# A three-way gate on ScalarE and VectorE: three activations per tile become two, and the maximum becomes a minimum and a maximum

## The chip, the core and the metric

One core of a Trainium2 chip runs the whole program. The metric is the device time of one execution in microseconds. TensorE (PE) multiplies matrices into PSUM, and its weight loads (PEld) are listed apart; ScalarE (ACT) and VectorE (DVE) work elementwise from PSUM or SBUF to SBUF; GpSimd (POOL) fills constants and issues some DMAs; SyncE (SP) issues most of them.

## What is computed

A linear attention with a delta rule over 768 steps gives `x`, 3072 tokens of 384 numbers. A feed-forward layer follows, whose activation has three pieces with `beta = 1`:

```python
h = x @ w_in                      # 3072 x 384 times 384 x 2048
neg = h <= -beta
pos = h >= beta
g = np.where(pos, h, np.where(neg, 0.0, (h + beta) ** 2 / (4.0 * beta)))
return (g @ w_out)                # 3072 x 2048 times 2048 x 384
```

With u = (h + 1) / 2 the middle piece is u squared. u squared is never below h, and it meets h at h = 1 and 0 at h = -1.

## The kernel before

The tokens come in six groups of 512. The attention of a group is made in chunks of 64 steps, by many small products (Gram matrices, a triangular solve on VectorE, a chain of state updates), and each result lands in a tile `xb` as a high and a low part. The feed-forward layer works on the group before: its 2048 hidden units are 16 tiles of 128. One *item* is one such tile for one group, 128x512 numbers; in the first group, 12 items are halves of 128x256. There are 102 items, 90 whole and 12 half.

For each item `up` makes `h` in PSUM (tile `h`, two buffers) with nine products (high and low parts of both factors, three passes over three tiles). The activation makes `s` in SBUF from `h`. `rest` splits `s` into a high part `ghi` (a cast on ScalarE, L807) and a low part `glo` (a subtraction on VectorE, L808), and `down`, two items later (`LAG = 2`), multiplies these with the second weight into the accumulators `o0` to `o3`.

The activation of an item before the change:

```python
relu(s[:, c], h[:, c], mid, -0.5)          # ScalarE, L812 called from L831
...
relu(s[:, c], s[:, c], one, -1.0)          # ScalarE, L812 called from L843
nc.scalar.activation(out=s[:, c], in_=s[:, c], func=AF.Square)                      # L844
...
nc.vector.tensor_tensor(out=s[:, c], in0=h[:, c], in1=s[:, c], op=ALU.max)          # L846
```

That is r = relu(0.5 - 0.5h), then relu(1 - r), which is u cut off below 0 and above 1, then its square, then the maximum with h.

The order of work on each engine is the order in which the code is written: the pools are under a manual schedule, each engine runs its instructions in that order, and semaphores make it wait. Pieces of the attention stand between the items: `pe` holds products for an item's two halves, whose evictions run on ScalarE and VectorE (`finish(evicts)` between the first relu and the second, `finish(late)` ahead of the next item), `fill` holds steps of the solve on VectorE and loads, and in the first group the letters of `FRONT` and `FILL` place the unpacking of the weights (a `grow` and a `cast` on ScalarE, `shift`, `join` and `low` on VectorE). Lines that come up below: L165 products on a zero tile that keep TensorE at work in the opening, L239 a Gram product of K, L370 a transpose of the solve's result into `XT`, L414 the write of the first merge into `XT`, L426 and L441 a product of the second merge and its eviction to `GG`, L476 the eviction to `SU`, L493 the product that reads `SU`, L693 `up`, L708 `down`, L324 and L368 two operations of the solve, L457 and L551 two of the state chain.

Of the kernel before, what the change touches and what calls it, by code (L numbers as in the profile page):

```python
# [7 lines left out]
F32 = mybir.dt.float32  # L8
F32R = mybir.dt.float32r
I32 = mybir.dt.int32  # L10
AF = mybir.ActivationFunctionType
ALU = mybir.AluOpType
# [28 lines left out]
def delta_rule_moe(ctx: ExitStack, tc: tile.TileContext, kqa, kqb, kv, beta, w, out):  # L41
# [14 lines left out]
    nc = tc.nc  # L56
# [5 lines left out]
    P = 128  # L62
# [3 lines left out]
    const = ctx.enter_context(tc.tile_pool(name="const", bufs=1))  # L66
# [104 lines left out]
                                channel_multiplier=-1, compare_op=ALU.is_gt, fill=0.0)  # L171
    mid = const.tile([P, 1], F32, name="half")
    nc.vector.memset(mid, 0.5)
    one = const.tile([P, 1], F32, name="one")
    nc.vector.memset(one, 1.0)
    tiny = const.tile([P, 1], F32, name="tiny")
    nc.vector.memset(tiny, 1e-30)  # L177
    nc.scalar.activation(out=sb.tile([P, 32], F32, name="y0")[:, 0:1], in_=mid, func=AF.Sqrt, bias=tiny)
# [406 lines left out]
    def finish(evicts):  # L585

        for p in [q() for q in evicts]:
            if p:
                p()

    def products(*pieces):
        return [p() for p in pieces]
# [29 lines left out]
    def do(codes):  # L622
        for c in codes:
            if c in "wW":
                weight_loads(tile_[0], tile_[0] + 1, nc.scalar if c == "W" else nc.sync)
                tile_[0] += 1
            elif c == "F":
                dense(1)
            elif c == "l":
                f, g = loads.pop(0)  # L630
                f(g)
            else:
                run(tasks[c], 1)
# [51 lines left out]
    def cols(bs):  # L685
        return slice(bs[0] * NB, bs[-1] * NB + NB)

    def up(G, f, bs):
        h = ps.tile([P, 2 * NB], F32, name="h", bufs=2)
        n = 0  # L690
        for k in range(3):
            for x, y in PASSES:
                nc.tensor.matmul(h[:, cols(bs)], WT[f][:, 0, x, k * P:(k + 1) * P], XB[G][:, y, k, cols(bs)], start=(n == 0), stop=(n == 8))  # L693
                n += 1
        return h

    def down(G, f, bs):
        ghi, glo = gs.pop((G, f, bs))
        for b in bs:
            left[G, b] -= 1  # L700
            for k in (2 * b, 2 * b + 1):
                if (G, k) not in oacc:
                    oacc[G, k] = ps.tile([P, DM], F32, name=f"o{k}")
                    new = True
                else:
                    new = False
                for n, (x, y) in enumerate(PASSES):
                    nc.tensor.matmul(oacc[G, k], (ghi, glo)[x][:, k * P:(k + 1) * P], WT[f][:, 1, y, :],  # L708
                                     start=(new and n == 0), stop=(left[G, b] == 0 and n == 2))

    def store(G, b):
        o = sb.tile([P, 2, DM], F32, name="wx", bufs=2)
        for k in (2 * b, 2 * b + 1):
            nc.scalar.copy(out=o[:, k % 2], in_=oacc[G, k])
            for j in range(CT):
                send(G, k, j, o, nc.sync)
# [79 lines left out]
    def fills(at_):  # L796
        for x, *n in fill.pop(at_, []):
            if x in (load_k, load_q, load_kv, weight_loads):
                x(*n)
            else:  # L800
                run(x, *n)

    def rest(item, s):
        ghi = sb.tile([P, 2 * NB], F32R, name="ghi", bufs=2)
        glo = sb.tile([P, 2 * NB], F32R, name="glo", bufs=2)
        c = cols(item[2])
        nc.scalar.copy(out=ghi[:, c], in_=s[:, c])  # L807
        nc.vector.tensor_tensor(out=glo[:, c], in0=s[:, c], in1=ghi[:, c], op=ALU.subtract)  # L808
        gs[item] = ghi, glo

    def relu(out, in_, bias, scale):
        nc.scalar.activation(out=out, in_=in_, func=AF.Relu, bias=bias, scale=scale)  # L812

    late, last, ready = [], None, []
    for n, item in enumerate(items):
        at_, c = 2 * n, cols(item[2])
        codes = FILL[n].split(",") if n < len(FILL) else [""] * 6
        do(codes[0])
        finish(late)
        do(codes[1])  # L820
        if last:
            rest(*last)
            ready.append(last[0])
        do(codes[2])
        if at_ == 2 * HALF:
            spare.clear()
        assert (item[1], low) in done, item
        h = up(*item)

        s = sb.tile([P, 2 * NB], F32, name="s", bufs=2)  # L830
        relu(s[:, c], h[:, c], mid, -0.5)  # L831
        evicts = products(*pe.pop(at_, []))
        do(codes[3])
        fills(at_)
        finish(evicts)
        do(codes[4])
        if len(ready) == LAG:
            x = ready.pop(0)
            down(*x)
            for b in x[2]:  # L840
                if left[x[0], b] == 0:
                    store(x[0], b)
        relu(s[:, c], s[:, c], one, -1.0)  # L843
        nc.scalar.activation(out=s[:, c], in_=s[:, c], func=AF.Square)  # L844
        late = products(*pe.pop(at_ + 1, []))
        nc.vector.tensor_tensor(out=s[:, c], in0=h[:, c], in1=s[:, c], op=ALU.max)  # L846
        do(codes[5])
        fills(at_ + 1)
        last = item, s
# [53 lines left out]
```

## Time and profile before

| | |
|---|---|
| three runs | 598.97, 602.3, 602.72 us; median 602.3 us |
| profiled execution, from the first to the last instruction | 599.7 us, its own time here |
| mean granted TensorE clock | 0.983 |
| TensorE busy | 581.0 us (97%) |
| its weight loads busy | 502.3 us (84%) |
| ScalarE busy | 396.5 us (66%) |
| VectorE busy | 394.2 us (66%) |

A busy time is the sum over an engine's instructions in that one execution. A wait is an engine's idle time ahead of an instruction, put down to what released it. Times in a listing are microseconds from the start of the span, and a line number is that of the kernel before.

### The profile page before, as it was taken

To read this page: it belongs to the slowest core of one execution; us is meant where nothing else is said; L and a number is where in the kernel's file an instruction comes from. 1 tells how busy PE (TensorE), PEld (TensorE's weight loads), DVE (VectorE), ACT (ScalarE), POOL (GpSimd) and SP (SyncE) were. 2 spreads that over 40 slices of the span, in tenths; PEclk is the share of its full clock that TensorE was granted. 3 is DMA by queue.
4 is the path that set the end of the run, shared out by engine and by line. 5 is a ranking of instruction groups with operands and counts; after the bars stand their busy time and mean duration, and the time that the engine had idled before them with its cause. 6 is when DMAs were issued, how large, how long until landed. Compare 5 with 4: busy or idle time off the path is not lost.

```text
span 599.7 us, 21759 instructions
## 1 busy us (share of the span) xinstructions
PE 581.0 (97%) x9585; PEld 502.3 (84%) x9585; DVE 394.2 (66%) x828; ACT 396.5 (66%) x689; POOL 33.0 (6%) x67
## 2 busy tenths in 40 slices
PE   8898999999999999999999999999999999999996
PEld 7777888788878878888888898888888888898986
DVE  5967899953689943689933689934689925333332
ACT  4538898478756596656586656586656585676663
POOL 6200010000020000020000020000020000000000
PEclk9969799999999999999999999999999999999999
DMA  5682657200333011134011134011143000020001
GB/s 144 207 290 86 205 194 210 66 8 9 93 96 103 8 32 45 31 98 121 13 32 45 33 103 119 8 32 45 34 108 91 1 3 16 15 54 1 0 1 52
DMA packets 32302, 42.77 MB, mean 71 GB/s; under 512 B 7056, under 2 KB 26768, under 8 KB 32208
## 3 DMA queue, kind: packets, MB, share of 16 engines
q1 hardware_dynamic: 31216, 40.41, 23.6%
q8 instruction: 75, 1.23, 0.9%
q0 software_dynamic: 576, 0.57, 0.4%
q10 hardware_dynamic: 416, 0.39, 0.2%
q14 instruction: 19, 0.16, 0.1%
HBM read 34.47 MB, written 4.72 MB: 65 GB/s over the span
## 4 chain that ended last, share of the span: by engine, by line
PE 46%; issue 28%; ACT 13%; DVE 5%; SPq 4%; DMA 3%; POOL 1%; POOLq 0%; ACTq 0%; DVEq 0%
PE o L708 16%; PE h L693 16%; PE ch L493 3%; ACT s L812 2%; ACT GG L441 2%; PE ch L467 2%; ACT XT L443 1%; PE o L165 1%; PE ch L252 1%; PE ch L451 1%; DMA KV<-in_kv_dram 1%; PE ch L566 1%; PE ch L428 1%; ACT s L844 1%; ACT xb L191 1%
## 5 line engine op out<-in xcount | busy, mean ns | idle before, releaser
L693 PE MATMUL h<-xb,wt 128*128 128x512 f32 (+1 forms) x918 | 225.0, 388 | 4.0 <-DVE s L846 2.0
L708 PE MATMUL o<-wt,ghi 128*128 128x384 f32 x768 | 200.7, 343 | 0.0
L693 PEld LDWEIGHTS h<-xb,wt 128*128 128x128 f32 x918 | 162.5, 189 | 38.1 <-DVE s L846 2.8
L708 PEld LDWEIGHTS o<-wt,ghi 128*128 128x128 f32 x768 | 137.8, 189 | 7.0
L846 DVE TENSOR_TENSOR s<-h,s 128x512 f32<-128x512 f32 (+1 forms) x102 | 66.8, 655 | 116.3 <-ACT s L844 115.4
L708 PE MATMUL o<-wt,glo 128*128 128x384 f32 x384 | 130.1, 339 | 0.3 <-DVE glo L808 0.3
L807 ACT CAST ghi<-s 128x512 fp32r<-128x512 f32 (+1 forms) x102 | 60.9, 597 | 102.9 <-DVE s L846 87.7
L808 DVE TENSOR_TENSOR glo<-s,ghi 128x512 fp32r<-128x512 f32 (+1 forms) x102 | 66.6, 653 | 39.2 <-ACT ghi L807 39.2
L812 ACT ACTIVATE s<-h,half 128x512 f32<-128x512 f32 (+1 forms) x102 | 67.4, 661 | 35.9 <-PE h L693 35.4
L708 PEld LDWEIGHTS o<-wt,glo 128*128 128x128 f32 x384 | 72.6, 189 | 1.1 <-DVE glo L808 1.1
L812 ACT ACTIVATE s<-s,one 128x512 f32<-128x512 f32 (+1 forms) x102 | 71.7, 703 | 2.4
L844 ACT ACTIVATE s<-s 128x512 f32<-128x512 f32 (+1 forms) x102 | 61.9, 607 | 3.2
L360 DVE TENSOR_TENSOR pr<-A 128x30 f32<-128x30 f32 (+14 forms) x120 | 39.3, 327 | 7.0 <-POOL A L325 5.1
L362 DVE TENSOR_TENSOR A<-A,pr 128x30 f32<-128x30 f32 (+14 forms) x120 | 39.8, 332 | 4.4
L165 PE MATMUL o<-wx 128*128 128x512 f32 x87 | 28.9, 479 | 1.5 <-DVE tiny L177 1.5
L493 PEld LDWEIGHTS ch<-Q,SU 64*64 64x64 f32 (+3 forms) x1056 | 22.4, 135 | 4.4 <-ACT ghi L807 1.5
L493 PE MATMUL ch<-Q,SU 64*64 64x64 f32 (+3 forms) x1056 | 24.7, 222 | 0.7 <-ACT SU L476 0.7
L165 PEld LDWEIGHTS o<-wx 128*128 128x128 f32 x87 | 18.8, 227 | 5.8 <-DVE tiny L177 1.5
L325 POOL TENSOR_SCALAR_AFFINE_SELECT A<-A 128x1024 f32<-128x1024 f32 x4 | 5.1, 1264 | 300.0 <-DMA xb<-X 256.4
L266 DVE TENSOR_TENSOR Q<-ch,mask 64x512 f32<-64x512 f32 (+1 forms) x30 | 20.6, 687 | 0.4
L426 PEld LDWEIGHTS ch<-XT,GG 32*32 32x32 f32 x704 | 12.4, 106 | 5.3 <-issue 2.8
L441 ACT ACTIVATE GG<-ch 32x512 f32<-32x512 f32 x22 | 12.9, 588 | 5.0 <-PE ch L426 4.7
(159 smaller groups left out, 575.2 us busy)
## 6 DMA issues: line engine op xcount, KB each, us to landing
wt<-in_w_dram SPq DMA_DIRECT2D x16, 768.0 KB, 6.0
out_dram<-wx SPq DMA_DIRECT2D x44, 96.0 KB, 2.2
KV<-in_kv_dram SPq DMA_DIRECT2D x36, 96.0 KB, 2.5
KV<-in_kv_dram SPq DMA_DIRECT2D x72, 48.0 KB, 2.4
KV<-in_kv_dram SPq DMA_DIRECT2D x12, 192.0 KB, 2.9
xb<-X SPq DMA_DIRECT2D x60, 32.0 KB, 2.0
K<-in_kqb_dram SPq DMA_DIRECT2D x12, 128.0 KB, 2.6
Q<-in_kqb_dram SPq DMA_DIRECT2D x12, 128.0 KB, 2.8
```

What stands on the lines that cost most here:

```text
L165: nc.tensor.matmul(warm_ps, warm[:, 0:P], warm, start=True, stop=True)
L360: nc.vector.tensor_tensor(out=pr, in0=A[:, 0:n, j:j + 1].broadcast_to([P, n, m]), in1=A[:, j:j + 1, j + 1:32].broadcast_to([P, n, m]), op= ...
L362: nc.vector.tensor_tensor(out=A[:, 0:n, j + 1:32], in0=A[:, 0:n, j + 1:32], in1=pr, op=ALU.add)
L441: nc.scalar.mul(out=GG[r:r + 32, ga, :, 0:32], in_=y1[r:r + 32], mul=-1.0)
L493: nc.tensor.matmul(yy[i][o * C:o * C + C, e, p], SF[rows, u:u + C], w_[rows, x, k, :], **how)
L693: nc.tensor.matmul(h[:, cols(bs)], WT[f][:, 0, x, k * P:(k + 1) * P], XB[G][:, y, k, cols(bs)], start=(n == 0), stop=(n == 8))
L708: nc.tensor.matmul(oacc[G, k], (ghi, glo)[x][:, k * P:(k + 1) * P], WT[f][:, 1, y, :], start=(new and n == 0), stop=(left[G, b] == 0 and n ...
L807: nc.scalar.copy(out=ghi[:, c], in_=s[:, c])
L808: nc.vector.tensor_tensor(out=glo[:, c], in0=s[:, c], in1=ghi[:, c], op=ALU.subtract)
L812: nc.scalar.activation(out=out, in_=in_, func=AF.Relu, bias=bias, scale=scale)
L844: nc.scalar.activation(out=s[:, c], in_=s[:, c], func=AF.Square)
L846: nc.vector.tensor_tensor(out=s[:, c], in0=h[:, c], in1=s[:, c], op=ALU.max)
```

## The change

The first relu takes the other sign of its scale, so that it gives relu(0.5h + 0.5), which is u cut off below 0 only. The second relu and its constant tile `one` are gone. The square is then taken of a number that may exceed 1, and VectorE takes the minimum of it with 1 ahead of the maximum with h, both in one scalar_tensor_tensor. In the changed kernel that operation stands on L840, the square on L838, the relu on L826.

```diff
-    one = const.tile([P, 1], F32, name="one")
-    nc.vector.memset(one, 1.0)
...
-    def relu(out, in_, bias, scale):
-        nc.scalar.activation(out=out, in_=in_, func=AF.Relu, bias=bias, scale=scale)
-
...
-        relu(s[:, c], h[:, c], mid, -0.5)
+        nc.scalar.activation(out=s[:, c], in_=h[:, c], func=AF.Relu, bias=mid, scale=0.5)
...
-        relu(s[:, c], s[:, c], one, -1.0)
         nc.scalar.activation(out=s[:, c], in_=s[:, c], func=AF.Square)
         late = products(*pe.pop(at_ + 1, []))
-        nc.vector.tensor_tensor(out=s[:, c], in0=h[:, c], in1=s[:, c], op=ALU.max)
+        nc.vector.scalar_tensor_tensor(out=s[:, c], in0=s[:, c], scalar=1.0, in1=h[:, c], op0=ALU.min, op1=ALU.max)
```

Engine by engine the instructions keep their order; 102 of ScalarE's and one memset of VectorE's are left out. One place stands for all: ScalarE's queue in the fifth group, from the eviction of the first merge to the evictions to `SU`. Before:

```order
L807 CAST ghi<-s 128x512
L812 ACTIVATE s<-h,half 128x512
L433 COPY XT<-ch 32x16x32 x2
L441 ACTIVATE GG<-ch 32x16x32 x2
L443 COPY XT<-XT 32x16x32 x2
L812 ACTIVATE s<-s,one 128x512
L844 ACTIVATE s<-s 128x512
L807 CAST ghi<-s 128x512
L812 ACTIVATE s<-h,half 128x512
L476 COPY SU<-ch 64x384 x2
```

And now, the same stretch:

```order
L805 CAST ghi<-s 128x512
L826 ACTIVATE s<-h,half 128x512
L431 COPY XT<-ch 32x16x32 x2
L439 ACTIVATE GG<-ch 32x16x32 x2
L441 COPY XT<-XT 32x16x32 x2
L838 ACTIVATE s<-s 128x512
L805 CAST ghi<-s 128x512
L826 ACTIVATE s<-h,half 128x512
L474 COPY SU<-ch 64x384 x2
```

The second relu between the eviction to `XT` and the square is left out; the rows around it keep their places.

## Rows read from the trace of the kernel before

**Rows 1.** The page, busy time of the engines.
```profile
PE 581.0 (97%) x9585; PEld 502.3 (84%) x9585; DVE 394.2 (66%) x828; ACT 396.5 (66%) x689; POOL 33.0 (6%) x67
```

**Rows 2.** Busy times by stretch: start:end, length, busy us of each engine.
```profile
52.00:594.90 542.90, 534.21 (x8508) 465.65 (x8506) 357.63 (x736) 369.12 (x640) 18.34 (x33) 0.99 0.21 58
...
75.00:120.00 45.00, 42.49 (x821) 35.86 (x817) 43.55 (x86) 32.87 (x55) 3.11 (x6) 1.00 0.50 156
180.00:210.00 30.00, 29.86 (x324) 26.21 (x322) 28.02 (x62) 16.99 (x27) 0.00 (x0) 1.00 0.22 55
```

**Rows 3.** TensorE's waits and their releasers: us in total, times, longest us.
```profile
PE h L693 <- DVE s L846: 2.0, 3, 1.0
...
PE ch L426 <- DVE XT L414: 1.1, 1, 1.1
PE ch L426 <- DVE XT L370: 0.9, 1, 0.9
...
PE ch L239 <- ACT GG L441: 0.8, 4, 0.3
PE ch L493 <- ACT SU L476: 0.7, 1, 0.7
```

**Rows 4.** ScalarE's groups by shape: busy us, mean ns, idle before.
```profile
L812 ACT ACTIVATE s<-s,one 128x512 f32<-128x512 f32 x90 | 65.5, 728 | 2.2
...
L812 ACT ACTIVATE s<-s,one 128x256 f32<-128x256 f32 x12 | 6.2, 513 | 0.2
```

**Rows 5.** VectorE's groups by shape.
```profile
L846 DVE TENSOR_TENSOR s<-h,s 128x512 f32<-128x512 f32 x90 | 61.7, 686 | 112.4 <-ACT s L844 111.7
...
L551 DVE TENSOR_TENSOR xb<-ch,xb 128x384 fp32r<-128x384 f32 x22 | 11.1, 547 | 0.0
L457 DVE TENSOR_TENSOR KV<-KV,ch 128x384 f32<-128x384 f32 x21 | 10.7, 547 | 1.7 <-PE ch L451 1.7
...
L368 DVE TENSOR_TENSOR A<-A,gm 128x1024 f32<-128x1024 f32 x4 | 4.9, 1220 | 0.0
L324 DVE SCALAR_TENSOR_TENSOR A<-A,gm 128x1024 f32<-128x1024 f32 x4 | 4.9, 1214 | 0.0
```

**Rows 6.** ScalarE in order of time at 488 us: start us, us, instruction.
```profile
488.15 0.72 ACT L812 ACTIVATE s<-s,one 128x512 f32<-128x512 f32 x1
...
491.58 1.45 ACT L476 COPY SU<-ch 64x384 f32<-64x384 f32 x3
```

**Rows 7.** ScalarE in order of time at 132 us.
```profile
132.15 0.72 ACT L812 ACTIVATE s<-s,one 128x512 f32<-128x512 f32 x1
...
134.75 1.19 ACT L441 ACTIVATE GG<-ch 32x512 f32<-32x512 f32 x2
```

**Rows 8.** VectorE in order of time at 207 us.
```profile
207.70 0.69 DVE L846 TENSOR_TENSOR s<-h,s 128x512 f32<-128x512 f32 x1 [0.18 <-ACT s L844]
```

**Rows 9.** TensorE's weight loads in order of time, near the end.
```profile
592.86 0.19 PEld L708 LDWEIGHTS o<-wt,glo 128*128 128x128 f32 x1 [0.17 <-DVE glo L808]
```

**Rows 10.** VectorE in order of time at 61 us.
```profile
61.18 0.42 DVE L846 TENSOR_TENSOR s<-h,s 128x256 f32<-128x256 f32 x1
...
62.39 0.41 DVE L414 TENSOR_TENSOR XT<-XT,o 128x256 f32<-128x256 f32 x1
```

**Rows 11.** Two of these stretches, L846 alone: start:end, length, VectorE busy, clock.
```profile
75.00:120.00 45.00, 4.94 (x8) 1.00 0.50 156
180.00:210.00 30.00, 4.79 (x7) 1.00 0.22 55
```

**Rows 12.** Stretches around a low clock; the third last column is the granted clock.
```profile
61.70:62.90 1.20, 0.10 (x3) 0.04 (x4) 1.17 (x3) 1.20 (x4) 0.00 (x0) 1.00 0.09 21
...
64.50:71.30 6.80, 6.75 (x82) 6.11 (x82) 6.68 (x14) 5.79 (x12) 0.00 (x0) 0.50 1.02 355
```

**Rows 13.** Chain that ended last, second relus: start us, us; first and last of 12.
```profile
53.42 0.52 ACT s L812
...
431.26 0.62 ACT s L812
```

## The prediction

> **What bounds the kernel now.** I read the page first: TensorE is busy 581.0 of 599.7 us, VectorE and ScalarE 66% each [rows 1]. The change takes work from ScalarE alone, so the question is where TensorE stands still, and for whom. The busy times by stage come next [rows 2]: from the first expert matmul at 52 us to the last at 594.9 us TensorE is busy 534.2 of 542.9 us. That leaves 8.7 us, and whatever a faster ScalarE gives has to come out of these 8.7 us or out of TensorE's clock. The same rows show who is nearly full: VectorE, with 43.55 of 45 us from 75 us on, 28.0 of 30 us from 180 us on, and three more such stretches in the later blocks. ScalarE has 17 of 30 us there. The list of TensorE's waits [rows 3] then names the releasers. The largest are VectorE's: its maximum `s` (L846) 2.0 us in three waits, its writes of `XT` 1.1 and 0.9 us. ScalarE's are small: the eviction to `GG` (L441) 0.8 us in four waits, the eviction to `SU` (L476) 0.7 us in one. So the removed row's engine is not the bound; I look at each wait and ask whether the removed row stands in the queue ahead of its releaser.
>
> **What is removed.** The second relu, 90 rows of 728 ns and 12 of 513 ns [rows 4], is 65.5 + 6.2 = 71.7 us of ScalarE's 396.5 us. The order of the instructions shows that nothing else moves on any engine, so each of these rows can shorten a wait only where it stands between a releaser and what that releaser waited for. The memset of `one`, one column on VectorE, goes too: TensorE's first products wait for loads that land after it, so I count nothing, and without that cover it would be one column's write. The first relu has another sign of its scale, one instruction with the same operands: no change.
>
> **What VectorE's new operation costs.** The trace has no minimum-and-maximum of one SBUF and one PSUM operand, so I bound it by the nearest rows [rows 5]. Today's maximum takes 686 ns for 128x512. That the PSUM operand becomes the second input and not the first changes nothing in the trace: 547 ns with PSUM second (L457), 547 ns with PSUM first (L551), both 128x384. That two operations with a scalar replace one changes nothing either: a scalar_tensor_tensor on 128x1024 takes 1214 ns (L324), a tensor_tensor on the same shape 1220 ns (L368). The lower end is therefore 6 ns in 1220, or 3 ns per operation and 0.3 us over 102 of them; the upper end is that the operation passes one element where today's passes two, which by L324 is 1214 ns. I take 686 ns, since L324 is the same instruction at the rate of a plain one; both ends come back below.
>
> The Trainium skill speaks against that: "Vector Engine (DVE) Microarchitecture Reference", section "Points that are easy to get wrong", says that a scalar_tensor_tensor with two SBUF sources that aren't bf16 runs at half the throughput. The trace does not agree for L324, which has two f32 sources in SBUF and is no slower than L368; and the new operation has only one source in SBUF. By that rule VectorE would get the load of the first rival below; by the row it gets none.
>
> **What it is worth, wait by wait.**
> - At 492 us TensorE waits 0.7 us for the eviction to `SU` [rows 3]. Back from it on ScalarE stand the first relu, the cast to `ghi` that waited for VectorE's maximum, the square, and the second relu at 488.15 us, with no wait for anything else between [rows 6]. All of them come about 0.75 us earlier, the row's 0.72 us and the gap behind it, and TensorE's products are there in time, so the 0.7 us go whole. Next in line is TensorE itself.
> - At 136 us the next Gram product waits 0.3 us (the longest of the four) for L441. The second relu at 132.15 us is two evictions ahead of it [rows 7]; the 0.3 us go. At the other three places the removed row stands behind the evictions in the queue, and they stay.
> - At 210.8 us the wait of 0.9 us is for VectorE's transpose L370, which follows the maximum at 207.70 us, which had waited 0.18 us for the square [rows 8]. Only these 0.2 us go; then VectorE's own queue is late.
> - At the end the last item's chain is bare: TensorE waits 0.17 us for `glo` at 592.86 us [rows 9]. The chain gets 0.75 us shorter, so 0.2 us go.
> - The waits for L846 (2.0 us) and for `XT` at 62.9 us (1.1 us) don't go. There VectorE runs one row after the other with hardly a gap: L846 at 61.18 us has no idle time noted before it, and the write of `XT` at 62.39 us comes when its queue gets to it [rows 10]. An earlier square only waits longer in that queue.
>
> The sum is 0.7 + 0.3 + 0.2 + 0.2 = 1.4 us. Everywhere else the removed 71.7 us lie beside a TensorE that has work. Against the profiled execution's own time, its span of 599.7 us, that gives 598.3 us. That execution was 2.6 us quicker than the median of the runs, 602.3 us, while the fastest of them took 598.97 and the slowest 602.72 us, so I put the forecast against the median: **600.9 us**, 0.2% less. Some 1% is what a measurement of this kernel can tell from no change.
>
> **Rivals.**
> 1. **The new operation runs at half rate.** Then each takes 1214 in place of 686 ns, 0.53 us more. From 180 to 210 us there are 7 of them [rows 11]: 3.7 us on a VectorE with 2.0 us free, so 1.7 us run over; four such stretches make 6.8 us. From 75 to 120 us 8 of them make 4.2 us with 1.45 us free: 2.8 us. TensorE needs each maximum to free one of its two `h` buffers, so the 9.6 us reach it: 602.3 - 1.4 + 9.6 = 610.5 us, slower. It decides from about 0.28 us more per operation (2.0 us over 7). L324 speaks against it, and only the page for it. Chance 0.05.
> 2. **TensorE's clock comes back.** From 64.5 to 71.3 us the granted clock is 0.50, the 1.2 GHz level, and TensorE is busy 6.75 us; just ahead, from 61.7 to 62.9 us, it was busy for 0.10 of 1.20 us [rows 12]. If the stall were gone and the clock stayed at 2.4 GHz, half of 6.75 us would be saved: 600.9 - 3.4 = 597.5 us. Against it: the stall ends with VectorE's write of `XT`, whose queue the change doesn't shorten. The other way round, another such low stretch would cost 3.4 us: 604.3 us. Chance 0.07 for the gain, 0.05 for the loss. The Trainium skill, "TensorE: Matmul & The Clock Gate", section "Part 1: The HAM clock gate (the "warmup" mystery)", has activity release the clock and idleness throttle it; the rows agree as to the order of stall and drop, and by that rule too it hangs on whether this stall goes.
> 3. **ScalarE's queue is the true path.** The chain that ended last runs through 12 second relus, from 0.52 us at 53.42 us to 0.62 us at 431.26 us, 7.6 us together [rows 13]. If each were worth its whole length: 602.3 - 7.6 = 594.7 us, faster by 1.3%. Against it: where the chain leaves TensorE for ScalarE, TensorE was busy all the while but for the 8.7 us [rows 2], of which VectorE, DMA and issue hold most. Chance 0.04.
>
> **How the numbers follow.** The forecast has 0.75, the rivals 0.05, 0.07, 0.05 and 0.04; 0.04 is left for cases that I don't see, half to each side. The range goes from the clock's gain, less the 0.3 us lower end of the new operation and some of the runs' own spread, to the clock's loss: 596.5 to 604.3 us. Faster by over 1% (below 596.3 us) is rival 3 and half of the rest: 0.06. Slower by over 1% (above 608.3 us) is rival 1 and the other half: 0.07. That leaves 0.87 within 1%.
>
> **What would show it.** ScalarE's busy time falls by some 72 us to about 325 us, VectorE's stays at 394 us, and the row at L840 takes 680 to 700 ns. TensorE's busy share stays at 97%. Its wait for `SU` at 492 us is gone, the waits for VectorE's maximum and for `XT` at 62 us stay, and so does the low clock behind the latter. VectorE's wait for the square, 111.7 us today [rows 5], shrinks by tens of us without a change of the span. The prediction is wrong if L840 takes far more than 0.69 us, if low-clock stretches come or go, or if TensorE's waits for VectorE shrink too, which would mean that VectorE's queue hung on ScalarE after all.

## The result, and the profile after

| | before | after |
|---|---|---|
| median of the runs taken together | 602.51 us (598.97 to 603.27, 4 runs) | 594.15 us (593.8 to 595.94, 4 runs) |
| ratio, 95% interval | | 0.9877 [0.9853, 0.9902] |
| the two once more, in a later comparison | 600.4 us (598.29 to 603.36, 18 runs) | 596.9 us (594.12 to 597.96, 6 runs) |
| ratio, 95% interval | | 0.9927 [0.9898, 0.9956] |
| profiled execution | 599.7 us | 592.5 us |

The kernel became faster, by 1.2% in the first comparison and by 0.7% in the second. I had forecast 0.2%, 600.9 us. The two intervals overlap. The traces below show a steady gain of 3.6 to 3.9 us behind the first 115 to 120 us; the rest of the first 8.4 us is put down to the scatter of those first us, which is there without the change too.

The page of the kernel after, busy time of the engines, and the shares of the chain that ended last:

```profile
PE 574.1 (97%) x9585; PEld 498.0 (84%) x9585; DVE 393.6 (66%) x827; ACT 327.3 (55%) x587; POOL 32.9 (6%) x67
...
PE 51%; issue 29%; DVE 11%; ACT 4%; SPq 2%; DMA 1%; POOL 1%; ACTq 0%; POOLq 0%; DVEq 0%
```

ScalarE loses 69.2 us against [rows 1], VectorE's busy time stays. VectorE's groups by shape, of the kernel after:

```profile
L806 DVE TENSOR_TENSOR glo<-s,ghi 128x512 fp32r<-128x512 f32 x90 | 61.8, 686 | 38.0 <-ACT ghi L805 37.9
L840 DVE SCALAR_TENSOR_TENSOR s<-s,h 128x512 f32<-128x512 f32 x90 | 61.4, 682 | 93.8 <-ACT s L838 93.8
```

The new operation takes 682 ns, where the old maximum took 686 [rows 5], and its wait for the square falls from 111.7 to 93.8 us. TensorE's waits after, as in [rows 3]:

```profile
PE h L691 <- DVE s L840: 1.9, 3, 1.0
...
PE ch L424 <- DVE XT L412: 0.8, 1, 0.8
...
PE ch L424 <- DVE XT L368: 0.7, 1, 0.7
...
PE ch L237 <- ACT GG L439: 0.3, 2, 0.2
```

The wait for `SU` is gone, those for VectorE's maximum and for `XT` at 62 us are still there. By this list TensorE gains little more than I had summed up. The list doesn't show where the rest came from, and the next view says why. From item 13's first product of `up` to the end of the last product, before and then after (start:end, length, busy us of PE, PEld, DVE, ACT, POOL, granted clock, DMA):

```profile
118.68:594.90 476.22, 471.99 (x7105) 412.35 (x7105) 294.45 (x615) 317.12 (x550) 15.76 (x28) 1.00 0.17 44
```

```profile
115.26:587.88 472.62, 470.14 (x7105) 412.05 (x7105) 294.03 (x615) 254.42 (x460) 15.73 (x28) 1.00 0.17 45
```

The stretch is 3.6 us shorter. But TensorE's *busy* time shrinks by 1.85 us in it, with the same 7105 products at the same clock: half of the gain came out of time that counted as busy. I call this stretch the **body** and what lies ahead of it the **opening**.

The body repeats from execution to execution; the opening doesn't. Lengths in us, from the traces:

| kernel | opening | body |
|---|---|---|
| before; the same again | 118.68; 115.71 | 476.22; 476.18 |
| after; the same again | 115.26; 116.72 | 472.62; 472.35 |

Within the body two places scatter between the two traces of the kernel before, by 0.46 us at 169 us and by 0.37 us, the other way, at 442 us; they are left out of the next table.

Setting the first product of every item beside its counterpart gives the places where the body shrinks. The steps are the same to 0.1 us in the four traces that have the new activation in every item and nothing put back. The last column holds what the forecast had for the place.

| at (us, before) | step, us | TensorE waited there for | forecast |
|---|---|---|---|
| 126 | 0.58 | VectorE's write of `XT` (L414) | - |
| 140 | 0.30 | eviction to `GG` (L441) | 0.3 |
| 166 | 0.30 | VectorE's `xb` (L551) | - |
| 212 | 0.24 | VectorE's transpose to `XT` (L370) | 0.2 |
| 227, 317, 406 | 3 x 0.42 | `gram_k`'s eviction (L243) inside the products of L467 | - |
| 263 | 0.13 | VectorE's maximum (L846) | - |
| 495 | 0.75 | eviction to `SU` (L476) | 0.7 |
| end | 0.13 | the last item's chain | 0.2 |

Together 0.58 + 0.30 + 0.30 + 0.24 + 1.25 + 0.13 + 0.75 + 0.13 = 3.68 us; the four that were forecast make 1.42 of it.

**The halt that the list of waits doesn't show.** TensorE's weight loads before, at 311 us in order of time, and ScalarE at the same place:

```profile
311.15 0.19 PEld L467 LDWEIGHTS ch<-KV,XT 64*64 64x64 f32 x4 [0.35 <-issue]
311.59 1.01 PEld L467 LDWEIGHTS ch<-KV,XT 64*64 64x64 f32 x60 [0.24 <-ACT GG L243]
```

```profile
309.05 0.72 ACT L812 ACTIVATE s<-s,one 128x512 f32<-128x512 f32 x1
309.80 0.63 ACT L844 ACTIVATE s<-s 128x512 f32<-128x512 f32 x1
310.46 1.07 ACT L243 COPY GG<-ch 128x512 f32<-128x512 f32 x2
```

And the same two after:

```profile
306.32 1.02 PEld L465 LDWEIGHTS ch<-KV,XT 64*64 64x64 f32 x64 [0.35 <-issue]
```

```profile
304.22 0.63 ACT L838 ACTIVATE s<-s 128x512 f32<-128x512 f32 x1
304.88 1.07 ACT L241 COPY GG<-ch 128x512 f32<-128x512 f32 x2
```

Before, 4 of 64 products start and the other 60 halt until `gram_k`'s eviction, which stands two rows behind the second relu, has emptied the accumulators: the group takes 311.59 + 1.01 - 311.15 = 1.45 us of loads. After, all 64 run in 1.02 us, 0.43 us less. In TensorE's own list the halt is not there, since the modelled ends of the first four products cover it; it stands only in the list of the *weight loads*. The same products in TensorE's list, before, in one piece:

```profile
311.15 1.57 PE L467 MATMUL ch<-KV,XT 64*64 64x48 f32 x64
```

**VectorE's queue hung on ScalarE.** VectorE before, behind item 12's second relu at 120.02 us, and TensorE's loads:

```profile
121.45 0.69 DVE L846 TENSOR_TENSOR s<-h,s 128x512 f32<-128x512 f32 x1 [1.44 <-ACT s L844]
...
124.57 0.41 DVE L414 TENSOR_TENSOR XT<-XT,ch 128x256 f32<-128x256 f32 x1
```

```profile
125.04 1.01 PEld L252 LDWEIGHTS ch<-Q,K 48*64 48x64 f32 x60 [0.38 <-DVE XT L414]
```

After:

```profile
117.27 0.69 DVE L840 SCALAR_TENSOR_TENSOR s<-s,h 128x512 f32<-128x512 f32 x1 [0.69 <-ACT s L838]
...
120.39 0.42 DVE L412 TENSOR_TENSOR XT<-XT,ch 128x256 f32<-128x256 f32 x1
```

```profile
121.03 1.02 PEld L250 LDWEIGHTS ch<-Q,K 48*64 48x64 f32 x64 [0.25 <-DVE XT L412]
```

The maximum waits for the square 0.69 in place of 1.44 us. All that is queued behind it, the write of `XT` among it, comes that much earlier, and the 64 products of L250 run without a halt in their midst.

### The profile page after: what moved, and what is told of

It reads as the page before. It is cut to its first block, busy times and chain, and to the rows that moved or that the text cites. A ratio compares the mean times of both kernels' runs of the same rounds, so it can differ in the third digit from the quotient of the medians.

```text
span 592.5 us, 21657 instructions
## 1 busy us (share of the span) xinstructions
PE 574.1 (97%) x9585; PEld 498.0 (84%) x9585; DVE 393.6 (66%) x827; ACT 327.3 (55%) x587; POOL 32.9 (6%) x67
## 4 chain that ended last, share of the span: by engine, by line
PE 51%; issue 29%; DVE 11%; ACT 4%; SPq 2%; DMA 1%; POOL 1%; ACTq 0%; POOLq 0%; DVEq 0%
PE h L691 18%; PE o L706 17%; PE ch L491 3%; PE ch L237 2%; PE ch L449 1%; PE ch L465 1%; PE o L165 1%; ACT GG L439 1%; PE ch L426 1%; DVE glo L806 1%; PE ch L250 1%; PE ch L564 1%; PE ch L424 1%; DVE wt L208 1%; DVE pr L347 1%
## 5 line engine op out<-in xcount | busy, mean ns | idle before, releaser
L840 DVE SCALAR_TENSOR_TENSOR s<-s,h 128x512 f32<-128x512 f32 (+1 forms) x102 | 66.4, 651 | 95.2 <-ACT s L838 95.2
L826 ACT ACTIVATE s<-h,half 128x512 f32<-128x512 f32 (+1 forms) x102 | 67.5, 662 | 61.0 <-PE h L691 60.5
L838 ACT ACTIVATE s<-s 128x512 f32<-128x512 f32 (+1 forms) x102 | 62.2, 610 | 2.4
L165 PE MATMUL o<-wx 128*128 128x512 f32 x87 | 27.8, 464 | 1.5 <-DVE tiny L175 1.5
L165 PEld LDWEIGHTS o<-wx 128*128 128x128 f32 x87 | 18.2, 220 | 5.7 <-DVE tiny L175 1.5
L474 ACT COPY SU<-ch 64x384 f32<-64x384 f32 (+1 forms) x30 | 14.3, 476 | 6.6 <-PE ch L465 6.3
L579 DVE TENSOR_TENSOR SU<-ch,SU 48x384 f32<-48x384 f32 (+1 forms) x27 | 15.0, 555 | 3.4 <-PE ch L564 3.0
```

The lines of the kernel that those rows point to most:

```text
L165: nc.tensor.matmul(warm_ps, warm[:, 0:P], warm, start=True, stop=True)
L826: nc.scalar.activation(out=s[:, c], in_=h[:, c], func=AF.Relu, bias=mid, scale=0.5)
L840: nc.vector.scalar_tensor_tensor(out=s[:, c], in0=s[:, c], scalar=1.0, in1=h[:, c], op0=ALU.min, op1=ALU.max)
```

## The experiments

In all of them the body, of one trace each, tells causes apart to some 0.5 us; medians, with the opening's scatter in them, do so to 2 or 3 us.

**The kernel before, unchanged.** No edit.

> The kernel before, unchanged, for its spread and the granted clock of each run. Theory Q (ScalarE's queue: each second relu shortened the way of later work, and the 8 us are small gains all along): all runs near 602 us, with the clock near 0.983 in each, as in its profile. Theory C (the clock's phase: the profiled run of before had three low stretches in the first 75 us, the changed kernel's two, 3.1 us of the difference stand before the first item, where both programs are alike): the runs scatter from 596 to 603 us, with clocks from 0.98 to 0.995, and the quick ones have the high clock.

Measured: ratio 1.0 [0.9977, 1.0023], 598.24 to 603.71 us in 12 runs, body 476.18 us. The low clock at 64.5 us [rows 12] is not there, although TensorE halts for `XT` just ahead of it as before. TensorE's row and the stretch behind it:

```profile
61.29 0.88 PE L426 MATMUL ch<-XT,GG 32*32 32x32 f32 x44 [0.96 <-DVE XT L414]
```

```profile
61.50:68.30 6.80, 6.00 (x150) 5.35 (x142) 6.68 (x14) 6.60 (x12) 0.00 (x0) 1.00 1.02 335
```

So one program has an opening of 118.68 us with this low stretch and one of 115.71 us without. What looked like a property of the kernel was one execution's. The runs scatter as theory C has it: the four quickest have clocks of 0.991 to 0.993, the three slowest 0.979 to 0.986. The low clock isn't the whole of the opening's scatter, though: two later traces with one stretch of 6.8 us at 0.50 each have openings of 115.30 us (half of some evictions moved) and 118.19 us (the constant tile kept).

**The constant tile kept.** After, with the unused `one` and its memset.

```diff
+    one = const.tile([P, 1], F32, name="one")
+    nc.vector.memset(one, 1.0)
```

> The changed kernel with the constant tile one and its memset kept, so that the opening on VectorE and every address behind that tile are those of before. If the opening's 3.1 us come from the memset or from the 32 bytes by which later tiles moved, the time goes back by about 3 us to 597; by theories Q and C it stays at 594 us.

Measured: 0.993 [0.9904, 0.9956], 596.72 us, body 472.36 us. The median is the 597 us of the memset's explanation, but the changed kernel itself, run again without the tile, has 596.9 us (below) and a body of 472.35 us. So the memset costs nothing in the body, and in the opening nothing that its scatter lets one see.

**The new activation in the first group alone, and in the later groups alone** (`item[0] > 0` in place of `item[0] == 0`).

```diff
+        new = item[0] == 0
+        relu(s[:, c], h[:, c], mid, 0.5 if new else -0.5)
...
+        if not new:
+            relu(s[:, c], s[:, c], one, -1.0)
...
+        if new:
+            nc.vector.scalar_tensor_tensor(out=s[:, c], in0=s[:, c], scalar=1.0, in1=h[:, c], op0=ALU.min, op1=ALU.max)
+        else:
+            nc.vector.tensor_tensor(out=s[:, c], in0=h[:, c], in1=s[:, c], op=ALU.max)
```

> The new activation in the first group's 22 items alone, the old one in the other 80. Theory Q: the gain of the items up to 170 us, which the two traces put at 0.9 us behind the clock's share, so 601 us. Theory C with a cause in the first items (an earlier activation there keeps TensorE from the stall that the low clock follows): 602.5 - 3.4 - 0.9, about 598 us, and a clock near 0.99.

> The old activation in the first group's 22 items, the new one in the other 80. Theory Q: the two traces drift apart by 2.9 us from 172 us to the end, so 599.5 us; the forecast on record gave these items 0.2 + 0.7 + 0.2 = 1.1 us, so 601.4 us. Theory C: the clock stays near 0.983.

Measured: 0.9963 [0.9936, 0.999] and 0.9954 [0.9936, 0.9972], medians 598.62 and 598.16 us against 600.9 us; bodies 475.52 and 473.59 us, 0.7 and 2.6 us under the kernel before. The medians alone don't choose: the first lies nearer theory C's 598 than theory Q's 601 us. In the body the gain is spread over both parts and nearly adds up (3.3 of 3.7 us; the first lacks 0.5 us for a pause at 134 us, which the runs with the relu in some of the items show again). It isn't one event, and not the clock's, which is 1.00 throughout the body.

**The second relu put back.** After, with a relu of bias 0 and scale 1 in the old place, so that ScalarE's load is the old one and VectorE keeps its new operation. The unchanged changed kernel ran beside it.

```diff
+        nc.scalar.activation(out=s[:, c], in_=s[:, c], func=AF.Relu, bias=zero, scale=1.0)
         nc.scalar.activation(out=s[:, c], in_=s[:, c], func=AF.Square)
```

> The changed kernel with an activation put back at the second relu's place, in place on s, that changes nothing (relu of a number that is not below 0, scale 1, bias from a tile of zeros). VectorE's new operation stays. Theory A (the row's place: it stood ahead of evictions and of the square on ScalarE's queue, and all of the gain behind 85 us comes from that): the 3.8 us behind 85 us are lost again, step by step (0.56 at 122 us, 0.3 at 137 us, 0.24 at 208 us, three of 0.42 at the state chain's first product, 0.75 at 492 us), and the median is that of before, about 601 us. A rival that VectorE's new operation has a share: some of the steps stay.

> The changed kernel once more, unchanged, in more runs. Its first four runs had a median of 594.15 us; the copy with the tile one kept had 596.72 us in six, with the same steps from 85 us to the end. If the two differ by chance in the opening (before 85 us), these runs have a median of 595.5 to 597 us and scatter by about 2 us; if the missing tile is worth something, they stay at 594 us.

Measured: 1.0009 [0.9981, 1.0037] with the relu, 0.9927 [0.9898, 0.9956] without; bodies 476.41 and 472.35 us. The gain in the body is the removed row's; VectorE's new operation costs nothing that shows there.

**The relu back in 11 items, in the other 91, and in 3.** The list in the diff is that of the 11. They are the items whose second relu stood ahead of a step in the table above; the 3 are those ahead of `gram_k`'s eviction at 227, 317 and 406 us.

```diff
+        if n in (12, 14, 19, 20, 29, 31, 37, 47, 63, 79, 101):
+            nc.scalar.activation(out=s[:, c], in_=s[:, c], func=AF.Relu, bias=zero, scale=1.0)
```

> The changed kernel, with one more row on ScalarE (a relu of s with bias 0 and scale 1, in place, where the second relu stood, 0.72 us) in 11 of the 102 items: 12, 14, 19, 20, 29, 31, 37, 47, 63, 79, 101. These are the items whose second relu stood just ahead of a step in the time by which the later items start earlier after the change. Theory Q (the row's place in ScalarE's queue: it counts only where it stands ahead of something that TensorE halts for) expects that these 11 rows take back all of it: from the first product of item 13 to the last product 476.2 to 476.5 us, as with the row in all items, against 472.4 us without. Theory L (ScalarE's load as such) expects 11 of 102 parts of the 4 us, 0.4 us: 472.8 us. The opening scatters by some us in both.

> The changed kernel, with the same added row in the other 91 items, 65 us of ScalarE's time. Theory Q expects that it costs nothing: 472.3 to 472.8 us from the first product of item 13 to the last product, and a median of 596 to 598 us. Theory L expects 91 of 102 parts of the 4 us: 475.9 us, and a median near 600 us.

> The changed kernel, with the same added row in three items, 31, 47 and 63, where gram_k's eviction stands behind it in ScalarE's queue and chain_u's products wait for that eviction. Theory Q expects three steps of 0.41 to 0.43 us, at the first products of items 33, 49 and 65, together 1.25 us, and nothing else: 473.6 us from item 13's first product to the last. If the pause inside chain_u's group is only one of the records, with no effect on the end, it stays at 472.4 us.

| relu in | ratio | median, us | body, us |
|---|---|---|---|
| 11 items | 0.997 [0.9946, 0.9995] | 599.91 | 476.17 |
| the other 91 | 0.9916 [0.9885, 0.9947] | 597.32 | 473.88 |
| 3 items | 0.9964 [0.9935, 0.9993] | 598.48 | 473.63 |

The kernel before had a median of 602.08 us in these runs, and of 600.4 and 600.9 us in the others; the body is the surer measure. Eleven rows, 7.5 us of ScalarE's time (its busy time is 334.8 against 327.3 us), bring the body back to that of the kernel before. Step by step they take back eight of the table's ten places, 3.2 us; the steps at 140 and 263 us don't come back, and a pause at 131 us that isn't theirs (below) makes up for them. The three rows take back 1.0 to 1.3 us, in three steps of 0.43, 0.42 and 0.41 us at the first products of items 33, 49 and 65; no other step behind item 23 is above 0.13 us. The pause is real time. With the relu back in item 47, ScalarE and TensorE's loads read as before the change:

```profile
306.92 0.72 ACT L841 ACTIVATE s<-s,zero 128x512 f32<-128x512 f32 x1
307.67 0.63 ACT L842 ACTIVATE s<-s 128x512 f32<-128x512 f32 x1
308.33 1.07 ACT L243 COPY GG<-ch 128x512 f32<-128x512 f32 x2
```

```profile
309.03 0.20 PEld L467 LDWEIGHTS ch<-KV,XT 64*64 64x64 f32 x4 [0.35 <-issue]
309.46 1.01 PEld L467 LDWEIGHTS ch<-KV,XT 64*64 64x64 f32 x60 [0.23 <-ACT GG L243]
```

The 91 rows, 62 us of ScalarE's time (389.3 against 327.3 us), come with 1.3 to 1.5 us more and not the nothing that I expected, though far from the 3.5 us of the load theory. 0.9 us of it comes at items 14 and 15, in two groups of TensorE's loads that stop for "issue" and for no engine:

```profile
125.03 0.31 PEld L252 LDWEIGHTS ch<-Q,K 48*64 48x64 f32 x12 [0.25 <-DVE XT L414]
125.58 0.89 PEld L252 LDWEIGHTS ch<-Q,K 48*64 48x64 f32 x52 [0.24 <-issue]
...
133.75 0.10 PEld L428 LDWEIGHTS ch<-GG 32*32 32x32 f32 x1 [0.40 <-issue]
```

The pause at L428 stands also in the trace with the 11 rows (0.38 us) and in that of the new activation in the first group alone (0.44 us), and the latter has no second relu in any item near it. So it isn't an added row's, and both sets carry it: that is part of why 3.7 and 1.4 us make more than the whole. Where these pauses come from stays open. Without the one at L428 at most some 1.0 us is left for the 91 rows, with the step at 263 us (0.13 us) among it.

**The relu in another place.** The same row in all items, but straight behind the first relu, ahead of the evictions.

```diff
         nc.scalar.activation(out=s[:, c], in_=h[:, c], func=AF.Relu, bias=mid, scale=0.5)
+        nc.scalar.activation(out=s[:, c], in_=s[:, c], func=AF.Relu, bias=zero, scale=1.0)
         evicts = products(*pe.pop(at_, []))
```

> The changed kernel, with the same added row in all items, but straight behind the first relu, ahead of the evictions of the attention's products (where it stood before it came behind them). ScalarE's load is that of the kernel before. Theory Q expects that every merge's evictions to XT and GG and the evictions to SU now come 0.7 us later, and that TensorE waits for more of them: at least 3 us more than with the row in its old place, 479 us or more from item 13's first product to the last, with the growth at the items where the merges stand. Theory L expects the 476.4 us of the row in its old place.

Measured: 1.006 [1.0039, 1.0081], 605.58 us, body 480.02 us. The load is that of the kernel before, and the place alone costs 3.6 us more. TensorE's waits in this kernel, against 0.8 and 0.7 us in [rows 3]:

```profile
PE ch L239 <- ACT GG L441: 2.9, 4, 0.9
...
PE ch L493 <- ACT SU L476: 1.4, 1, 1.4
```

**The cast made twice.** After, with `ghi` written twice, 0.62 us more for each whole item.

```diff
         nc.scalar.copy(out=ghi[:, c], in_=s[:, c])
+        nc.scalar.copy(out=ghi[:, c], in_=s[:, c])
```

> The changed kernel with the cast to ghi made twice: some 64 us more of work for ScalarE, nearly as much as the second relu was, but behind the evictions of the item before and ahead of the first relu. Theory A: the three steps of 0.42 us at the state chain's first product stay (its accumulators are freed by an eviction that is ahead of the added cast), the 0.75 us at 492 us are lost for the most part (there the eviction to SU stands behind it), and so is the 0.3 us of the end: about 1.2 us over the changed kernel. Theory L (ScalarE's load as such): nine tenths of the 3.8 us are lost, 3.4 us over the changed kernel.

Measured: 1.0121 [1.0098, 1.0145], 608.38 us, body 483.47 us, 11.1 us over the changed kernel. Neither theory had the size. VectorE's `glo` waits for `ghi`, and VectorE's queue waits with it. Its group, and TensorE's largest wait:

```profile
L807 DVE TENSOR_TENSOR glo<-s,ghi 128x512 fp32r<-128x512 f32 x90 | 61.9, 688 | 64.1 <-ACT ghi L806 63.0 <-PE ch L449 0.6
```

```profile
PE ch L424 <- DVE XT L368: 5.5, 4, 1.6
```

`glo` waits 63.0 where it waited 37.9 us, so the solve's last transpose L368 comes late, four times, once in each of the later groups, and TensorE's products of L424 stand for it 5.5 us. Item by item most of the growth lies at these merges, 0.4 to 1.5 us at a time. The granted clock falls to 0.50 of full speed, the 1.2 GHz level, for two more stretches, from 394.4 and from 486.5 us, 1.2 and 1.8 us behind such a halt (1.33 us up to 393.14 us, 1.17 us up to 484.78 us). The first products of items 64 and 80, right behind these stretches, come 1.33 and 1.50 us later each, those of items 32 and 48, at the same places of other groups without the low clock, 0.62 and 0.61 us: an estimate of 1.6 us for the clock. Most of the rest lies in the halts at the merges.

**Half of some evictions moved to VectorE.** After, with half of the second merges' evictions and of `gram_k`'s on VectorE, to see whether ScalarE's queue is still late anywhere.

```diff
-                nc.scalar.copy(out=(GE[g - 2] if g in (2, 3) else GG[:, g % 2])[:, half(f)], in_=b_[f])
+                (nc.vector.tensor_copy if g > 3 and f else nc.scalar.copy)(out=(GE[g - 2] if g in (2, 3) else GG[:, g % 2])[:, half(f)], in_=b_[f])
...
+                    if split and r:
+                        nc.vector.tensor_scalar(out=GG[r:r + 32, ga, :, 0:32], in0=y1[r:r + 32], scalar1=-1.0, scalar2=None, op0=ALU.mult)
```

> The changed kernel with half of the evictions of the second merge and of the later Gram products of K on VectorE, which has under 6 of 15 us of work at these places (210, 300 and 390 us). Theory A: the waits that are left there, 0.16 to 0.18 us ahead of the Gram product and what the state chain's first product still loses, go, about 0.2 to 0.4 us in each of four groups, 1 us in all. A rival is that VectorE's queue delays these halves behind a scaling that waits for a load: then it is slower by up to 1 us.

Measured: 0.9902 [0.9868, 0.9936], 594.43 us, against 0.9927 [0.9898, 0.9956] for the changed kernel in the same runs. The intervals overlap; the body is 472.00 against 472.35 us, and the difference is one step at 169 us, a place that scatters by itself. The waits that were to go are still there, now for VectorE's half:

```profile
PE ch L237 <- DVE GG L440: 0.5, 3, 0.2
```

The two halves of the second merge's eviction to `GG` run one behind the other: at 301 us ScalarE's runs from 301.19 for 0.59 us, and VectorE's starts at 301.81 us. So the edit didn't bring this eviction's end forward, and whether an earlier end would gain anything stays open.

## Why the prediction was wrong

- **The failed step** is "Everywhere else the removed 71.7 us lie beside a TensorE that has work". The four terms came nearly as forecast, 0.75, 0.30, 0.24 and 0.13 us for 0.7, 0.3, 0.2 and 0.2; but four kinds of places had been left out, worth 0.58 + 0.30 + 1.25 + 0.13 = 2.26 us. The sum of 1.4 us should have been 3.7 us, and the forecast then 598.6 us.
- That would have been within the range of 596.5 to 604.3 us, and so is the second comparison's 596.9 us. That the first comparison's 594.15 us lies below it is by the opening's scatter, as far as the traces show; no run shows another cause.
- Over half of the 2.26 us, 1.25 us, is the halt inside L467's products. It was missed because I read TensorE's waits alone. The weight loads' list of the kernel before has it. Its group of this shape, in the trace of before:

```profile
L467 PEld LDWEIGHTS ch<-KV,XT 64*64 64x64 f32 x640 | 11.0, 134 | 3.5 <-issue 2.7 <-ACT GG L243 0.7
```

  The same group after has no ScalarE behind it:

```profile
L465 PEld LDWEIGHTS ch<-KV,XT 64*64 64x64 f32 x640 | 10.4, 134 | 2.8 <-issue 2.6
```

- "That leaves 8.7 us, and whatever a faster ScalarE gives has to come out of these 8.7 us or out of TensorE's clock" was wrong for the same reason: busy time has halts in it, and 1.85 us of the 3.6 us came out of it.
- "An earlier square only waits longer in that queue" holds for the waits that the prediction named: the maximum's three have 1.9 us after for 2.0 us before, and the one for `XT` at 62 us, 1.1 us, still has 0.8. At 126 and 166 us, where it didn't look, it doesn't hold: there the maximum, at the head of VectorE's queue, was itself waiting for the square, 1.44 and 1.36 us before and 0.69 and 0.94 us after. The prediction named this as what would prove it wrong, "that VectorE's queue hung on ScalarE after all".
- The three other places of L239's wait stayed, as said: the items behind them start no earlier, though the list after names only two of the three.
- "TensorE's first products wait for loads that land after it" was misread: the trace before puts the 1.53 us ahead of its first products, those on the zero tile (L165), down to VectorE's opening memsets. The count of nothing for the memset was right even so: they start at 1.53 us after the change too.
- **The new operation's price** was right: 682 ns for a forecast of 680 to 700. The first rival is out. VectorE's wait for the square fell by 17.9 us, less than the tens of us that were forecast. The Trainium skill's rule ("Vector Engine (DVE) Microarchitecture Reference", section "Points that are easy to get wrong") of half throughput for two SBUF sources that aren't bf16 doesn't reach this operation, whose one source lies in PSUM.
- **The clock**, the second rival: the low stretch at 64.5 us is gone in the trace after, but it is gone as well from the kernel before, run again, with the same halt ahead of it. It belongs to the opening's scatter and not to the change. That scatter, 115.3 to 119.8 us over the fourteen traces, without order by kernel, fits the part of the first 8.4 us that the second comparison didn't repeat.
- **The third rival**, ScalarE's queue as the path, had the mechanism nearest to the truth and too large a price: the chain's 12 second relus, 7.6 us. The gain per place is bounded by what is late next, 0.13 to 0.75 us, and only part of the chain's places carry one.

What stays open is why the opening's low clock falls where it does in one execution and not in another, and what else makes the opening scatter.

## What to carry to other kernels

When a row is taken off an engine, walk its queue and look behind each such row for the first thing that another engine needs, an eviction that frees an accumulator above all, and follow it through a second engine's queue too. For TensorE read the waits of the weight loads beside those of the products: a group that starts a few products and then stops counts as busy. A row's place decides its price: the same row in all items cost 4 us in one place and 7.6 us in another, and of the 4 us the rows of eleven items alone made 3.2.

## What the runs showed of the hardware

- A group of 64 small products that halts after its fourth shows no idle time in TensorE's own list, but 0.24 us and an unexplained 0.35 us in its weight loads' list; 0.42 us of real time go by. The 0.35 us "issue" ahead of the group is there with and without the halt.
- A scalar_tensor_tensor of minimum and maximum with one PSUM source costs 682 ns for 128x512, what a plain tensor_tensor costs.
- The granted clock of one program differs between executions in the first 100 us: with a halt of TensorE of 1.10 and 0.96 us at 61 to 63 us it was 0.50 right behind it in one trace and 1.00 in another, and the opening differed by 3.0 us.
